# Attention and two expert layers on one core: the first chunk of expert 0 inside the attention stage, routing in groups of 4, 5, 5 and 4 token tiles with two under way

## The chip, the cores and the metric

The kernel runs on one core of one Trainium2 chip. The metric is the device time of one execution in microseconds; lower is better. TensorE (PE) multiplies and transposes, VectorE (DVE) and ScalarE (ACT) read and write the matmul memory PSUM, GpSimd (POOL) works between tiles in on-chip memory and issues gathers, and SyncE (SP) issues all other DMAs. Each engine runs its instructions in the order in which the program emits them.

## What is computed

An attention with pooled keys and values is followed by two mixtures of experts. The inputs are 4 batches, 8 heads, 576 positions and 64 dimensions, so 2304 tokens of 512 values.

```python
k_p = k.reshape(B, H, S//8, 8, D).mean(axis=3); v_p = the same of v
attn = softmax(q @ k_p.T / sqrt(D));  x = attn @ v_p        # [2304, 512]
noisy = x @ w_gate + log1p(exp(x @ w_noise)) * noise        # 8 experts
top2, weights = two largest of noisy, softmax over the two
out1[token] = sum over its two experts of weight * (relu(x @ w1[e]) @ w2[e])   # F = 1024
out2 = sum over 4 experts of p[:, e] * (relu(out1 @ w1b[e]) @ w2b[e])          # dense
```

## The kernel before

The attention works on 18 tiles of 128 tokens, each in two units of four heads, so 36 units; `LAG` is 5. Iteration `i` of the loop at line 651 emits for PE the scores of unit `i`, the transposes of the exponentials of unit `i - 2` and the values of unit `i - 5`. Between them `soft` emits for DVE the maximum of unit `i`, and the reciprocal and the products of unit `i - 6` (`normalise`: one product for x, one for the gate columns). The exponential is ACT's; in every fourth unit DVE first subtracts the maximum into the tile `sh`. After every tile its x goes to DRAM (`x_d`) and its gate logits to `lg`. Iterations 36 to 41 have no scores left; `warm` emits three filler matmuls in each of them (line 658).

`routing(g, hold)` (line 322) is a generator that turns the logits of a group of tiles into places in the experts' token lists: softplus noise, the two largest (`max`, `max_index`), one-hot tiles, counts by matmul (`pos`), positions, one-hot tiles again (`oh_hi` for the list's block, `oh_lo` for the row in it), and their product by matmul into a table (`tab`), which is added to `slotf`. Each `yield` ends one step; `step` (line 446) runs some steps of the first generator in the list `bg`, between the other work. The groups are tiles 0-3, 4-8, 9-11 and 12-17, one after another. A `yield` with a value holds the generator until that many further calls. After the second group the first two blocks of the lists of experts 0 and 1 are known (`slots[False]`), and POOL gathers their rows of `x_d` (`fetch1`, line 569). After the last group the others are fetched.

Then come the experts. A chunk of tokens is worked in two halves of F. Each half has four layer-1 units (line 718: 12 matmuls each, three terms of a split into high and low parts) and a layer-2 sum per 128 tokens (line 782: 12 matmuls of 512 columns). ACT writes the relu's high part, DVE the low part (`relu_split`). `run_plain` (line 817) runs a chunk; the first two chunks have 256 tokens, the first of expert 0 and of expert 1. Weights come in items of 512 KB: SP loads one into one of three staging tiles, ACT copies its high part and POOL (in some places DVE) subtracts for the low part (lines 506 to 518), into rings of three places for layer 1 and three for layer 2, the third of which lies in memory that the attention uses. Items 0 to 4 are split during the attention (line 643), the others beside the chunks (`ahead_plain`, line 795). `turn_plain` (line 587) turns gathered tiles with PE and splits them: ACT the high part, DVE the low part. At line 673 the attention's memory is closed and the tiles of the expert stage take its place.

What the steps of the prediction touch: the loop (651 to 668), `soft`, `transposes`, `normalise` (249 to 304), `routing` and `step` (322 to 455), `relu_split` and `layer1` (706 to 729), lines 669 to 673, and the first two calls of `run_plain` (955 to 962).

Of the kernel before, what the change touches and what calls it, by code (L numbers as in the profile page):

```python
# [22 lines left out]
J = S // POOL  # L23
# [12 lines left out]
GROUPS = (0, 4, 9, 12, NT)  # L36
EARLY = 2
LAG = 5
STEPS = (4, 4, 2, 3, 3, 5, 5, 4, 4)
GN = 6  # L40
# [15 lines left out]
def tile_attention_moe_moe(  # L56
# [93 lines left out]
    for t in et_sb:  # L150
# [7 lines left out]
                   base=0, channel_multiplier=0, allow_small_or_imprecise_dtypes=True)  # L158
    exp_i = consts.tile([128, E1], FT, name="exp_i")
# [75 lines left out]
    sps, es, ets, xs, lgm, pvs = {}, {}, {}, {}, {}, {}  # L235
# [13 lines left out]
    def soft(i, j):  # L249
# [21 lines left out]
    def transposes(i):  # L271
# [4 lines left out]
        nc.scalar.activation(ets[i][:J], p[:J], AF.Copy)  # L276
# [12 lines left out]
    def normalise(i, rec):  # L289
        t, g = divmod(i, 2)  # L290
        p3 = pvs[i]
        if g == 0:
            xs[t] = wk.tile([128, DM], FT, name="xs", bufs=6)
            lgm[t] = wk.tile([128, H, 2 * E1], FT, name="lgm", bufs=2)
        nc.vector.tensor_tensor(xs[t][:, g * 256:(g + 1) * 256].rearrange("p (h d) -> p h d", d=D),
                                p3[:, :, 0:D], rec.unsqueeze(2).to_broadcast([128, 4, D]), op=OP.mult)
        step()
        nc.vector.tensor_tensor(lgm[t][:, 4 * g:4 * g + 4, :], p3[:, :, D + 1:VW],
                                rec.unsqueeze(2).to_broadcast([128, 4, 2 * E1]), op=OP.mult)
        step()  # L300
        if g == 1:
            nc.sync.dma_start(x_d[t * 128:(t + 1) * 128, :], xs[t])
            nc.vector.tensor_reduce(lg[:, t, :], lgm[t].rearrange("p h c -> p c h"),
                                    axis=AX.X, op=OP.add)
# [16 lines left out]

    def routing(g, hold):
# [5 lines left out]

        def w(name, c=E1, d=FT):
            return consts.tile([128, GN, c], d, name="g_" + name)[:, :n]  # L330
# [7 lines left out]
        yield  # L338
        nc.scalar.activation(ln, u, AF.Ln)
# [3 lines left out]
        nc.vector.tensor_scalar(u, z, 0.0, None, op0=OP.max)  # L343
        yield
        nc.vector.tensor_sub(ln, ln, d)
        yield
        nc.vector.tensor_add(ln, ln, u)
# [19 lines left out]
        yield hold[0]  # L367
        pos = psr.tile([128, 512], FT, name="tr")
# [14 lines left out]
        nc.vector.tensor_add(base, base, cnt)  # L383
        yield
# [17 lines left out]
        lo = consts.tile([128, GN, 2, 128], HF, name="oh_lo")[:, :n]  # L402
        hi = consts.tile([128, GN, 2, HC], HF, name="oh_hi")[:, :n]
# [15 lines left out]
        yield hold[3]  # L419
        if a:  # L420
# [13 lines left out]
        if g == EARLY - 1:  # L434
            nc.vector.tensor_tensor(base, base, least, op=OP.max)
            yield
        if last:
            nc.vector.tensor_reduce(top_n, base, axis=AX.X, op=OP.max)
            nc.vector.tensor_scalar(over, top_n, float(CAP), None, op0=OP.is_gt)
            yield  # L440

    bg = []

    held = [0]
# [179 lines left out]

    at(2, pool_v, 0)
# [14 lines left out]
    at(28, make_va, 3)  # L640
    for g in range(len(GROUPS) - 2):
# [473 lines left out]
```

## Time and profile before

| | us |
|---|---|
| median of 3 runs | 1330.58 |
| lowest, highest | 1327.60, 1330.93 |
| the profiled execution | 1331.74 |
| its span, first to last instruction | 1329.90 |

All durations below are of that one profiled execution. Its last scores start at 83.39 us after the span's start, the first chunk's layer 1 at 104.92, the second chunk at 129.14 and the third at 161.39. In the views, "idle" is time in which an engine had nothing to run, with what ended it; the granted clock is a share of TensorE's 2.4 GHz, the lower of its two levels being 1.2 GHz, so a mean between 0.5 and 1 is a mix of both. Matmuls overlap at their ends: the distance from one group's start to the next says what the first costs.

### The profile page before, as it was taken

How to read it: one execution, taken by the hardware profiler on the slowest of the kernel's cores; microseconds unless marked ns; L12 is line 12 of the kernel's file. 1: busy time of each engine (PE TensorE's matmuls, PEld its weight loads, DVE VectorE, ACT ScalarE, POOL GpSimd, SP SyncE). 2: the span in 40 equal slices, each digit the busy share in tenths (PEclk: the TensorE clock that was granted, in tenths of full speed). 3: DMA queues.
4: the chain of work that ended last, by engine and by line, in shares of the span. 5: the costliest groups of instructions: out<-in, count | busy, mean ns of one | idle time of the engine just before them, and what ended most of it. 6: DMA issues, size and time to landing. Idle time of an engine off the chain costs nothing.

```text
span 1329.9 us, 19627 instructions
## 1 busy us (share of the span) xinstructions
PE 1302.2 (98%) x7430; PEld 1160.0 (87%) x7430; DVE 729.4 (55%) x1361; ACT 571.1 (43%) x1039; POOL 848.2 (64%) x761
## 2 busy tenths in 40 slices
PE   8898999999999999999999999999999999999998
PEld 6767898899889988898888998999999889999997
DVE  6886525475675732567545457545444574444444
ACT  6754445556454544554433334434333433333331
POOL 6725588897977945423967666767566566655560
PEclk9999999999999999999999999999999999999999
DMA  9643565342424424663333223323221232222211
GB/s 364 220 144 93 162 201 179 110 153 95 150 96 136 156 90 131 218 205 119 115 95 94 81 64 118 121 64 111 73 70 64 64 111 74 70 72 71 64 33 48
DMA packets 48805, 156.19 MB, mean 117 GB/s; under 512 B 5952, under 2 KB 7744, under 8 KB 47552
## 3 DMA queue, kind: packets, MB, share of 16 engines
q1 hardware_dynamic: 42624, 134.94, 30.9%
q0 software_dynamic: 6080, 19.93, 4.7%
q8 instruction: 61, 1.00, 0.3%
q14 instruction: 40, 0.33, 0.1%
HBM read 134.92 MB, written 19.92 MB: 116 GB/s over the span
## 4 chain that ended last, share of the span: by engine, by line
PE 57%; DVE 3%; ACT 1%; DMA 0%; issue 0%; ACTq 0%; DVEq 0%
PE p L789 29%; PE wn L743 23%; PE wn L726 4%; DVE x L618 1%; PE tr L577 1%; DVE acc L1029 0%; DMA gat<-y_d,rows 0%; ACT hs L709 0%; ACT x L615 0%; DVE hs L710 0%; DVE gat L885 0%; DVE sx L607 0%; DVE wn L773 0%; DVE wn L764 0%; DVE v L518 0%
## 5 line engine op out<-in xcount | busy, mean ns | idle before, releaser
L743 PE MATMUL wn<-x,u 128*128 128x384 f32 (+1 forms) x2688 | 452.4, 327 | 0.2 <-ACT u L755 0.2
L743 PEld LDWEIGHTS wn<-x,u 128*128 128x128 f32 x2688 | 445.5, 188 | 2.9 <-ACT u L755 0.4
L789 PE MATMUL p<-v,hs 128*128 128x512 f32 x1776 | 438.4, 393 | 3.5 <-ACT hs L709 2.0
L789 PEld LDWEIGHTS p<-v,hs 128*128 128x128 f32 x1776 | 329.9, 188 | 75.6 <-ACT hs L709 4.5
L709 ACT ACTIVATE hs<-wn 128x384 fp32r<-128x384 f32 (+2 forms) x320 | 147.1, 468 | 280.9 <-DVE wn L764 146.2
L789 PE MATMUL p<-v_last,hs 128*128 128x512 f32 x912 | 235.0, 393 | 0.8 <-DVE acc L1029 0.5
L710 DVE SCALAR_TENSOR_TENSOR hs<-wn,hs 128x384 fp32r<-128x384 f32 (+2 forms) x320 | 163.9, 528 | 128.9 <-ACT hs L709 122.2
L789 PEld LDWEIGHTS p<-v_last,hs 128*128 128x128 f32 x912 | 170.9, 189 | 36.8 <-DVE acc L1029 1.0
L1029 DVE SCALAR_TENSOR_TENSOR acc<-p,pe,acc 128x512 f32<-128x512 f32 x126 | 94.5, 750 | 188.8 <-PE p L789 186.6
L518 POOL TENSOR_TENSOR v<-w_st,v 128x1024 fp32r<-128x1024 f32 x41 | 101.8, 2484 | 120.9 <-ACT v L512 120.8
L541 POOL TENSOR_TENSOR u<-comb,u 128x1024 fp32r<-128x1024 f32 x60 | 149.6, 2494 | 44.6 <-ACT u L535 44.2
L533 POOL TENSOR_TENSOR u<-w_st,u 128x768 fp32r<-128x768 f32 x60 | 114.0, 1900 | 49.1 <-ACT u L527 49.1
L512 ACT ACTIVATE v<-w_st 128x1024 fp32r<-128x1024 f32 x64 | 67.5, 1056 | 168.6 <-PE p L789 165.4
L726 PE MATMUL wn<-x,u 128*128 128x384 f32 (+1 forms) x768 | 125.0, 320 | 1.6 <-DVEq L1001 1.4
L726 PEld LDWEIGHTS wn<-x,u 128*128 128x128 f32 x768 | 120.9, 193 | 3.9 <-issue 1.8
L516 POOL TENSOR_TENSOR u<-w_st,u 128x256 fp32r<-128x256 f32 x80 | 59.6, 776 | 52.4 <-ACT u L512 32.0
L518 POOL TENSOR_TENSOR v_last<-w_st,v_last 128x1024 fp32r<-128x1024 f32 x22 | 55.2, 2510 | 47.9 <-ACT v_last L512 47.9
L535 ACT ACTIVATE u<-comb 128x1024 fp32r<-128x1024 f32 x64 | 67.5, 1054 | 29.1 <-POOL comb L525 29.1
L758 DVE TENSOR_TENSOR u<-wn,u 128x384 f32<-128x384 f32 (+1 forms) x64 | 34.4, 537 | 73.9 <-PE wn L743 39.2
L522 POOL TENSOR_TENSOR comb<-w_st 128x256 f32<-128x256 f32 x64 | 49.6, 775 | 36.2 <-DMA w_st<-wb 34.1
L512 ACT ACTIVATE v_last<-w_st 128x1024 fp32r<-128x1024 f32 x32 | 33.7, 1055 | 78.1 <-PE p L789 75.0
L565 POOL DMA_INDIRECT gat<-y_d,rows x36 | 36.9, 1026 | 36.7 <-DVE hs L710 13.6
(142 smaller groups left out, 1317.5 us busy)
## 6 DMA issues: line engine op xcount, KB each, us to landing
w_st<-wb SPq DMA_DIRECT2D x104, 512.0 KB
w_st<-wa SPq DMA_DIRECT2D x88, 512.0 KB
y_d<-acc SPq DMA_DIRECT2D x40, 256.0 KB
x_d<-xs SPq DMA_DIRECT2D x18, 256.0 KB
out<-acc SPq DMA_DIRECT2D x18, 256.0 KB
k_st<-kt SPq DMA_DIRECT2D x3, 1152.0 KB
v_st<-vt SPq DMA_DIRECT2D x3, 1152.0 KB
q_sb<-qt SPq DMA_DIRECT2D x3, 1152.0 KB
```

Of the source, the lines that this page charges most:

```text
L512: nc.scalar.activation(w[:, 0], st, AF.Copy)
L516: eng.tensor_sub(w[:, 1, i], st[:, i], w[:, 0, i].bitcast(FT))
L518: eng.tensor_sub(w[:, 1], st, w[:, 0].bitcast(FT))
L533: nc.gpsimd.tensor_sub(w[:, 1, 0:3], st[:, 1:4], w[:, 0, 0:3].bitcast(FT))
L535: nc.scalar.activation(w[:, 0, 3:7], t, AF.Copy)
L541: nc.gpsimd.tensor_sub(w[:, 1, 3:7], t, w[:, 0, 3:7].bitcast(FT))
L709: nc.scalar.activation(hi, p, AF.Relu)
L710: return lambda: nc.vector.scalar_tensor_tensor(hs[:, 1, f, c0:c0 + n], p, 0.0, hi.bitcast(FT), op0=OP.max, op1=OP.subtract)
L726: nc.tensor.matmul(p, w[:, a, qu, (kd % 2) * 128:(kd % 2 + 1) * 128], xc[(xa, xb)[kd // 2]][:, b, kd % 2, :n], start=i == 0, stop=i == 11)
L743: nc.tensor.matmul(p, w[:, a, wm, kd * 128:(kd + 1) * 128], xc[xm][:, b, kd, :n], start=first and i == 0, stop=i == 5, skip_group_check=True)
L789: nc.tensor.matmul(p, hs[:, a, f, t * 128:(t + 1) * 128], w[:, b, f % 2], start=f == 0 and i == 0, stop=f == FB // 2 - 1 and i == 2)
L1029: nc.vector.scalar_tensor_tensor(a, p, w, a, op0=OP.mult, op1=OP.add)
```

## The change

- Groups are tiles 0-3, 4-8, 9-13 and 14-17. `step` may go on with a second group while the first is held; a turn counter keeps their sums in order, and odd and even groups have work tiles of their own. More steps are taken in each iteration (`STEPS`), and holds last one call.
- `LAG` is 4. In every fourth unit the exponential is taken by the copy after the transposes. From tile 6 on x and gate columns are one product, and x is stored from a tile whose rows hold them side by side, 64 values of every 81.
- Routing's absolute value is ACT's, log(1 + e) is one ACT instruction with a bias, and two DVE instructions are merged into one.
- The first two gathered tiles of expert 0 are turned in iteration 35. The first four layer-1 units stand between the values of iterations 36 to 39 in place of the fillers. Layer 2 and the second half follow the loop, with a routing step of six after each; the result of both halves is summed in PSUM. Weight items 5 to 9 are split there. The last group starts right after the loop.
- The attention's memory is closed after that chunk. The second chunk reads its x from other tiles, and `run_plain` is called for it first. `combine_weights` becomes the end of the last group.

```diff
-GROUPS = (0, 4, 9, 12, NT)
+GROUPS = (0, 4, 9, 14, NT)
-LAG = 5
-STEPS = (4, 4, 2, 3, 3, 5, 5, 4, 4)
-GN = 6
+LAG = 4
+STEPS = (4, 4, 5, 5, 6, 7, 7, 6, 6)
+GN = (5, 5)
+JOINED = 6
...
-                sh = wk.tile([128, 4, J], FT, name="sh")
-                nc.vector.tensor_sub(sh, sps[i], mx.unsqueeze(2).to_broadcast([128, 4, J]))
-                nc.scalar.activation(es[i], sh, AF.Exp)
+                nc.vector.tensor_sub(es[i], sps[i], mx.unsqueeze(2).to_broadcast([128, 4, J]))
...
-        nc.scalar.activation(ets[i][:J], p[:J], AF.Copy)
+        nc.scalar.activation(ets[i][:J], p[:J], AF.Copy if i % 4 else AF.Exp)
...
+        if t >= JOINED:
+            x = xs[t].rearrange("p (h c) -> p h c", c=VW)
+            gates, x = x[:, :, D + 1:VW], x[:, :, 0:D]
+            nc.vector.tensor_tensor(xs[t].rearrange("p (h c) -> p h c", c=VW)[:, 4 * g:4 * g + 4, :], p3,
+                                    by.to_broadcast([128, 4, VW]), op=OP.mult)
...
-            nc.sync.dma_start(x_d[t * 128:(t + 1) * 128, :], xs[t])
+            nc.sync.dma_start(x_d[t * 128:(t + 1) * 128, :].rearrange("p (h d) -> p h d", d=D), x)
...
-        nc.vector.scalar_tensor_tensor(az, z, -1.0, z, op0=OP.mult, op1=OP.max)
-        yield
+        nc.scalar.activation(az, z, AF.Abs)
         nc.scalar.activation(ex, az, AF.Exp, scale=-1.0)
-        yield
+        nc.scalar.activation(ln, ex, AF.Ln, bias=one)
+        yield 0 if last else 1
...
+        while turn["base"] != g:
+            yield 1
...
-        while bg and n:
-            try:
-                if held[0]:
-                    held[0] -= new
-                    return
-                held[0] = next(bg[0]) or 0
-                n -= 1
-            except StopIteration:
-                bg.pop(0)
+        for r in list(bg):
+            if held.get(r):
+                held[r] -= new
+                continue
+            while n and not held.get(r):
+                try:
+                    held[r] = next(r) or 0
+                    n -= 1
+                except StopIteration:
+                    bg.remove(r)
+                    break
...
+    def first1(q, f):
+
+        layer1(q, f, S1, S2, FIRST, lambda: ps.tile([128, 512], FT, name="s"), h_first[q])
+        w_at["used1"] += f % 2
+
+    def first2(q, i):
+
+        if not y_first:
+            y_first.extend(ps.tile([128, 512], FT, name="et") for _ in range(FIRST // 128))
+        s = 4 * q + 2 + i
+        w_check(s)
+        w = w_slot(s)
+        for f in range(2):
+            for t in range(FIRST // 128):
+                for j, (a, b) in enumerate(TERMS):
+                    nc.tensor.matmul(y_first[t], h_first[q][:, a, 2 * i + f, t * 128:(t + 1) * 128], w[:, b, f],
+                                     start=q == i == f == j == 0, stop=q == i == f == 1 and j == 2,
+                                     skip_group_check=True)
+        w_at["used2"] += 1
+
+    def first_out(t):
+        y = wk.tile([128, H * VW], FT, name="xs", bufs=5)[:, 0:DM]
+        nc.scalar.activation(y, y_first[t], AF.Copy)
+        nc.sync.dma_start(y_d[t * 128:(t + 1) * 128, :], y)
...
+    for c in range(FIRST // 128):
+        at(35, turn_plain, (0, c), (S1, S2), c)
...
-        at(2 * GROUPS[g + 1] + LAG, lambda g=g: bg.append(routing(g, ((2, 1, 6, 1), (2, 1, 1, 1), (2, 1, 2, 1))[g])))
+        at(2 * GROUPS[g + 1] + LAG, lambda g=g: bg.append(routing(g, (1, 1, 1, 1))))
...
-        if i >= NI:
-            warm(3, ps, "s")
         if LAG <= i < NI + LAG:
             values(i - LAG)
+        if NI <= i < NI + 4:
+            first1(0, i - NI)
...
-    until(lambda: False in slots)
-    for c in range(FIRST // 128):
-        turn_plain((0, c), (S1, S2), c)
-    warm(4, ps, "s")
+    bg.append(routing(len(GROUPS) - 2, (1, 1, 1, 1)))
+    w_whole(5)
+    first2(0, 0)
+    step(6, 1)
+    first2(0, 1)
+    step(6, 1)
+    for f in range(FB // 2):
+        first1(1, f)
+        step(6, 1)
+        if f < 2:
+            w_whole(6 + f)
+        else:
+            turn_plain((1, f - 2), (A22, S4), f - 2)
+    for i in range(2):
+        first2(1, i)
+        w_whole(8 + i)
+        step(6, 1)
+    for t in range(FIRST // 128):
+        first_out(t)
+    until(lambda: turn["done"] > EARLY)
     att.close()
...
-    bg.append(routing(len(GROUPS) - 2, (3, 1, 1, 2)))
-    bg.append(combine_weights())
...
-    for c in range(2):
-        add(0, 1 + c, turn_plain, (1, c), (A11, S3), c)
-    run_plain(S1, S2, FIRST, sink1(0, 0), fills, 7)
-    fills.clear()
...
-        add(1, 3 + c, turn_plain, (0, 2 + c), (A22, S4), c)
-    run_plain(A11, S3, FIRST, sink1(1, 0), fills, 7, nc.gpsimd, nc.vector)
+        add(1, 3 + c, turn_plain, (0, 2 + c), (A11, S3), c)
+    run_plain(A22, S4, FIRST, sink1(1, 0), fills, 7, nc.gpsimd, nc.vector)
...
-    run_plain(A22, S4, CA, sink1(0, FIRST), fills)
+    run_plain(A11, S3, CA, sink1(0, FIRST), fills)
```

## Rows read from the trace of the kernel before

**Rows 1.** Stretches: length, busy PE, PEld, DVE, ACT, POOL (instructions), granted clock, DMA share, GB/s.
```profile
50.00:100.00 50.00, 43.15 (x552) 33.55 (x547) 41.66 (x174) 29.54 (x90) 20.38 (x28) 0.97 0.42 133
...
130.00:139.00 9.00, 5.30 (x34) 4.52 (x33) 6.97 (x13) 1.64 (x4) 1.79 (x3) 0.65 0.62 193
...
161.00:1329.00 1168.00, 1158.79 (x6063) 1045.32 (x6061) 615.03 (x962) 479.91 (x784) 762.87 (x621) 1.00 0.33 106
83.40:161.40 78.00, 69.01 (x499) 56.34 (x498) 47.93 (x170) 30.73 (x64) 34.96 (x46) 0.91 0.38 125
```

**Rows 2.** One stretch, the filler matmuls of line 465 alone: PE, PEld, clock, DMA.
```profile
83.40:161.40 78.00, 7.41 (x22) 2.19 (x22) 0.91 0.38 125
```

**Rows 3.** PE in order of time: start, us, instruction; iterations 34 to 36.
```profile
81.55 0.76 PE L245 MATMUL s<-kb,q_sb 128*128 128x144 f32 x4
...
82.67 0.79 PE L284 MATMUL pv<-va,et 128*64 128x81 f32 x16
83.39 0.76 PE L245 MATMUL s<-kb,q_sb 128*128 128x144 f32 x4
...
86.97 0.79 PE L284 MATMUL pv<-va,et 128*64 128x81 f32 x16
```

**Rows 4.** PE in order of time, the first chunk.
```profile
104.92 1.86 PE L726 MATMUL wn<-x,u 128*128 128x256 f32 x12
...
111.96 5.74 PE L789 MATMUL p<-v,hs 128*128 128x512 f32 x24
117.54 5.91 PE L726 MATMUL wn<-x,u 128*128 128x256 f32 x48
...
129.14 1.59 PE L726 MATMUL wn<-x,u 128*128 128x256 f32 x12
```

**Rows 5.** PE in order of time, the second chunk and the third's start.
```profile
133.39 1.25 PE L417 MATMUL tr<-oh_hi,oh_lo 128*128 128x40 f16 x8 [2.66 <-DVE oh_lo L410]
...
135.74 6.20 PE L726 MATMUL wn<-x,u 128*128 128x256 f32 x36
...
147.85 4.47 PE L726 MATMUL wn<-x,u 128*128 128x256 f32 x36
152.16 0.60 PE L577 MATMUL tr<-ident,gat 128*128 128x128 f32 x4
152.51 1.68 PE L726 MATMUL wn<-x,u 128*128 128x256 f32 x12
...
161.39 2.79 PE L726 MATMUL wn<-x,u 128*128 128x384 f32 x15
```

**Rows 6.** DVE in order of time: one-hot tiles of two groups.
```profile
54.47 2.59 DVE L410 TENSOR_TENSOR oh_lo<-slot_i,g_sf 128x256 f16<-128x256 f16 x3
...
85.68 1.09 DVE L410 TENSOR_TENSOR oh_lo<-slot_i,g_sf 128x256 f16<-128x256 f16 x3
```

**Rows 7.** Groups of instructions: busy us, mean ns, idle before; DVE's gate product.
```profile
L298 DVE TENSOR_TENSOR lgm<-pv,rec 128x64 f32<-128x64 f32 x36 | 7.7, 214 | 0.0
```

**Rows 8.** POOL in order of time, weight splits of the first chunk.
```profile
113.62 2.82 POOL L516 TENSOR_TENSOR u<-w_st,u 128x256 fp32r<-128x256 f32 x4 [18.99 <-PE p L789]
...
120.58 2.85 POOL L516 TENSOR_TENSOR v<-w_st,v 128x256 fp32r<-128x256 f32 x4
```

**Rows 9.** ACT in order of time, the copy of a weight item as it lands.
```profile
127.38 1.06 ACT L512 ACTIVATE v<-w_st 128x1024 fp32r<-128x1024 f32 x1 [1.76 <-DMA w_st<-wa]
```

**Rows 10.** ACT in order of time, the splits of a turned tile.
```profile
100.09 0.38 ACT L584 ACTIVATE x<-tr 128x256 fp32r<-128x256 f32 x1 [7.56 <-PE tr L577]
101.03 0.38 ACT L584 ACTIVATE x<-tr 128x256 fp32r<-128x256 f32 x1 [0.56 <-DVE x L585]
```

**Rows 11.** Stretches as in rows 1, with the stores of two tiles.
```profile
98.00:100.00 2.00, 2.00 (x29) 1.40 (x29) 1.83 (x8) 0.00 (x0) 0.00 (x0) 1.00 0.34 131
100.00:101.00 1.00, 0.05 (x1) 0.00 (x0) 0.42 (x1) 0.38 (x1) 0.00 (x0) 1.00 0.68 262
```

**Rows 12.** Groups of instructions: ACT's table load.
```profile
L128 ACT ACT_TABLE_LOAD x1 | 1.3, 1283 | 0.7 <-PEq L1107 0.7
```

More of the change, by code (lines that the diff above doesn't have):

```diff
@@ L158, in tile_attention_moe_moe @@
                    base=0, channel_multiplier=0, allow_small_or_imprecise_dtypes=True)
+    one = consts.tile([128, 1], FT, name="one")
+    nc.vector.memset(one, 1.0)
     exp_i = consts.tile([128, E1], FT, name="exp_i")
@@ L383, in routing @@
         nc.vector.tensor_add(base, base, cnt)
+        if g == EARLY - 1:
+            nc.vector.tensor_tensor(base, base, least, op=OP.max)
+        turn["base"] += 1
         yield
@@ L419, in routing @@
         yield hold[3]
+        assert turn["slot"] == g
+        turn["slot"] += 1
         if a:
@@ L440, in routing @@
             yield
+            yield from combine_weights()
+        turn["done"] += 1
     bg = []
-    held = [0]
+    held = {}
     def step(n=1, new=0):
-        while bg and n:
-            try:
-                if held[0]:
-                    held[0] -= new
-                    return
-                held[0] = next(bg[0]) or 0
-                n -= 1
-            except StopIteration:
-                bg.pop(0)
+        for r in list(bg):
[9 more added lines that the diff above has]
+                    break
     def until(done):
@@ L622, in x_both, with relu_split, pair_weights, bank @@
         x_lo(m, n)
+    TERMS = ((0, 0), (0, 1), (1, 0))
+    hid = []
+    def relu_split(f, c0, n, p, hs=None):
+        hs = hs or hid[0]
+        hi = hs[:, 0, f, c0:c0 + n]
+        nc.scalar.activation(hi, p, AF.Relu)
+        return lambda: nc.vector.scalar_tensor_tensor(hs[:, 1, f, c0:c0 + n], p, 0.0, hi.bitcast(FT),
+                                                      op0=OP.max, op1=OP.subtract)
+    def pair_weights(q, pr):
+        s = 4 * q + pr
+        w_check(s)
+        return w_slot(s)
+    def bank():
+        return pm.tile([128, 512], FT, name="wn", bufs=4)
+    def layer1(q, f, xa, xb, n, bank=bank, hs=None):
+        w = pair_weights(q, f // 2)
+        p = bank()[:, :n]
+        i = 0
+        for a, b in TERMS:
+            for kd in range(KD):
+                qu = (0 if f % 2 else 1) if kd < 2 else (3 if f % 2 else 2)
+                nc.tensor.matmul(p, w[:, a, qu, (kd % 2) * 128:(kd % 2 + 1) * 128],
+                                 xc[(xa, xb)[kd // 2]][:, b, kd % 2, :n], start=i == 0, stop=i == 11)
+                i += 1
+        relu_split(f, 0, n, p, hs)()
+    h_first, y_first = [], []
+    def first1(q, f):
[5 more added lines that the diff above has]
+        s = 4 * q + 2 + i
+        w_check(s)
+        w = w_slot(s)
[10 more added lines that the diff above has]
+        nc.sync.dma_start(y_d[t * 128:(t + 1) * 128, :], y)
     at(2, pool_v, 0)
@@ L702, in combine_weights @@
         yield
-    TERMS = ((0, 0), (0, 1), (1, 0))
-    def relu_split(f, c0, n, p):
-        hi = hs[:, 0, f, c0:c0 + n]
-        nc.scalar.activation(hi, p, AF.Relu)
-        return lambda: nc.vector.scalar_tensor_tensor(hs[:, 1, f, c0:c0 + n], p, 0.0, hi.bitcast(FT),
-                                                      op0=OP.max, op1=OP.subtract)
-    def pair_weights(q, pr):
-        s = 4 * q + pr
-        w_check(s)
-        return w_slot(s)
-    def layer1(q, f, xa, xb, n):
-        w = pair_weights(q, f // 2)
-        p = pm.tile([128, 512], FT, name="wn", bufs=4)[:, :n]
-        i = 0
-        for a, b in TERMS:
-            for kd in range(KD):
-                qu = (0 if f % 2 else 1) if kd < 2 else (3 if f % 2 else 2)
-                nc.tensor.matmul(p, w[:, a, qu, (kd % 2) * 128:(kd % 2 + 1) * 128],
-                                 xc[(xa, xb)[kd // 2]][:, b, kd % 2, :n], start=i == 0, stop=i == 11)
-                i += 1
-        relu_split(f, 0, n, p)()
     def layer1_seven(q, pr, n, fills, u):
@@ L749, in go @@
                 f()
-        p1, p6, p7, p5 = (bank() for _ in range(4))
+        p1, p6, p7, p5 = (bank()[:, :n] for _ in range(4))
         s1, u2, u3 = (moe.tile([128, CA], FT, name=f"u{i}")[:, :n] for i in range(3))
```

47 lines of the change are left out of this document (23 added, 24 removed).

## The prediction

> **What bounds the kernel now.** I read the view of stretches first, to see where TensorE (PE) falls short. From the third chunk on (161 us to the end) PE is busy 1158.79 of 1168 us at a granted clock of 1.00; nothing is to be had there, and what this change moves lies ahead of that mark. From the last scores to that mark, 83.4 to 161.4, it is busy 69.01 of 78.00 us at a mean clock of 0.91 [rows 1], and 7.41 us of that are the filler matmuls that only keep it active [rows 2]. So 78 us are spent on about 55 us of wanted work. PE's order of time then says where. In iteration 35 the values start at 86.97, where the pace would give 84.5 [rows 3]. The first chunk's layer 1 starts only at 104.92 and the chunk ends at 129.14, nearly without a pause [rows 4]. The second chunk (129.14 to 161.39) holds a 2.66 us wait for DVE's one-hot tiles, and then 36 matmuls take 6.20 us that take 4.47 later, the clock being 0.65 over 130 to 139 [rows 1, 5]. That wait is group 3's routing. Everything here is measured between two marks: the scores of iteration 35 (83.39) and the first 384-column matmul of the third chunk (161.39), 78.0 us apart.
>
> **What PE has to do between the marks afterwards.** Iteration 35 without a wait is one pace, 83.39 - 81.55 = 1.84 us, of which the values are 83.39 - 82.67 = 0.72 [rows 3]. After it stand four values (2.9) and two sets of transposes (at most the pace less the values, 1.1 for both). Seven gathered tiles are turned, at 152.51 - 152.16 = 0.35 each: 2.5 [rows 5]. Chunks 1 and 2 are four halves: 48 layer-1 matmuls at the pace of 36 in 152.16 - 147.85 = 4.31, so 5.75 [rows 5], and 24 layer-2 matmuls in 117.54 - 111.96 = 5.58 [rows 4]; four times 11.33 is 45.3. Routing matmuls of two groups: 1.5, from one group's 8 in 1.25 [rows 5]. Sum 55.1. The fillers, six trailing iterations without other work, and the first chunk's standing alone are gone: 78.0 - 55.1 = 22.9 us if PE never waits. What it will wait for has to come off that.
>
> **The waits, part by part.**
> (a) Routing inside the attention. Counting the yields, group 1's slots come out in iteration 32 instead of 36, its one-hots in 28 and 29 instead of 34, and group 2 is at its counts by 35 instead of 39. The 2.1 us that iteration 35 lost (86.97 less 84.5 and its 0.33 of table matmuls) is DVE running late with group 1's one-hots [rows 3]; it moves ahead of the first mark. But there POOL is splitting weights: three one-hot instructions took 2.59 us beside POOL's split against 1.09 without [rows 6]. Ends: 0, if the gaps of the earlier iterations take it, to 4.2, twice the loss. I take 2.1. In the other direction 24 units lose DVE's small gate product, 0.21 us each [rows 7], for a longer joint one, and four groups lose two small DVE instructions: 0 to 1 us, taken as 0, since these iterations' DVE work is not what PE waits for in most of them.
> (b) Before the first unit. The two gathers are issued in iteration 32, three paces or 5.5 us before they are turned. The nearest landing in the trace is a 512 KB weight load: released by POOL's end at 123.43, its copy could start at 127.38, so 3.95 us [rows 8, 9]. That leaves 1.5 us, less if stores and loads share the engines; 0.7, ends 0 and 4.7. Then four splits alternate between ACT and DVE, 0.94 us apart (101.03 is 0.56 of waiting for DVE and then 0.38 [rows 10]): about 3.4 us, of which turning, transposes and values cover 1.6. That makes 1.8. Together 2.5, ends 0 and 6.5.
> (c) Clock. A stretch with waits of this size was followed by the lower level, 1.2 GHz, and 36 matmuls cost 6.20 - 4.47 = 1.7 us more [rows 5]. One such fall: 1.7; ends 0 and 3.4.
> (d) First chunk. Units 0 to 3 need weights that are split long before. Item 5 can be split once the loop is over: POOL has 18.99 us of idle time there now [rows 8]. Items 6 and 7 must wait for the first layer-2 steps to free their places and are split in 2.85 us each [rows 8], ready about 1.5 us before use. 0.8 for group 2's table and a late weight; ends 0 and 3.
> (e) Second chunk. Group 3's four one-hots run beside POOL's splits at 0.86 us each [rows 6] and their table is wanted by unit 3, after three units of 1.44: 1.9 us late, and 0.3 for a relu behind a weight copy. 2.2; ends 1 and 7.8, the present loss of this chunk (32.25 less 24.4).
> Costed at nothing: the output of the first chunk (two ACT copies of PSUM at its end; cover: the second chunk's first two units write other banks; price without it about 1 us, like the splits), the Abs on ACT, and w_load behind the stores on SP, which waits for POOL anyway.
> Waits 9.3 in all (1.0 to 24.9), gain 22.9 - 9.3 = **13.6 us**.
>
> **Two prices that no row shows.** From iteration 18 the stores of x leave in 256-byte pieces. Over 98 to 101 two stores held the 16 engines 0.68 us each [rows 11]. If a small piece cost as long as a 2 KB one, a store would take eight times that, 5.4 us; if its bytes decided, 0.68. The share of 0.42 over 50 to 100 leaves 29 us free [rows 1], 37 with the twelve present stores taken out, so they fit up to 3.1 us each. I take them to fit, as nearer to the lower end by bytes. The Trainium skill (DMA: Bandwidth & Descriptors, Specifications) wants 512 bytes or more for line rate, since a smaller write is read, modified and written; its section on why small descriptors are slow adds 27% for 256 bytes. By that page a store would take an estimated 2 x 1.27 x 0.68 = 1.7 us, twelve 21 us, and they would fit. A second: Abs stands in no row. If it switched ACT's table and back in each group, 8 loads of 1.28 us [rows 12] would be up to 10 us of ACT time, mostly beside PE work; the other end is 0, which I take because Relu, Copy, Exp and Ln already share the single load. The Trainium skill (ScalarE: Activation LUTs, Table sets: the hidden batching unit) lists abs among the functions that every set holds; by it the price is 0.
>
> **The rivals.**
> A, the waits as above: 13.6 us. B, PE hardly waits: DVE's savings and early gathers leave (b) at 1.8 and (e) at 1, gain about 20, 1310.6. For it: over 50 to 100 DVE is busy 41.66 of 50 us and ACT 29.54 [rows 1]. Against: DVE is the late engine wherever PE waits now.
> C, weights take the place of routing. Four items of 2.85 us of POOL per half are 11.4 [rows 8], and PE takes 11.33 per half: level. If item 6's late place leaves POOL idle for 4 us and three gathers (2.9) stand between its splits, the first two chunks are paced by POOL; 6.9 of the gain is lost, 1324.
> D, the other side: the stores of small pieces. Above 3.1 us each they no longer fit; at 5.4 the twelve need 65 us where 37 are free, and gathers and weights come 28 us late: 1317 + 28 = 1345. It begins to cost more than the gain at about 4.2 us a store. Against it: the share of bytes.
> E, the change doesn't do what it says: group 1 comes too late, so that the chunk doesn't fit between the last values. The late end of (b) costs 4.0 more, a second fall of the clock 1.7, group 3 that much later 1.9: gain 6.0, 1324.6.
>
> **How the numbers follow.** The profiled execution took 1331.74 us (span 1329.90, 1.84 around it), 1.16 above the median of 1330.58. Against its own time A gives 1331.74 - 13.6 = 1318.1; against the median 1317.0, which I give. A's own range is 1312 to 1322 (waits 5 to 14). Chances: A 0.58, B 0.12, C 0.14, E 0.08, D 0.08. The range is 1309 to 1326: A, B and most of C and E, leaving out D and their ends. A measurement of this kernel tells 0.3%, 4 us, from no change, so faster means below 1326.6: A, B, 0.09 of C, 0.05 of E make 0.84; the remains of C and E, 0.08, are the same; D, 0.08, is slower.
>
> **What would show it.** After: layer-1 matmuls between the values of iterations 32 to 35; no filler at the end; the third chunk's first 384-column matmul 56 to 70 us after the scores of iteration 35, about 64. (a) scores of iteration 35 near 85.5; (b) PE's wait ahead of its first unit, 1 to 3 us, named after the gather or the split; (e) a wait for one-hots under 2.5 us in chunk 2. The prediction is wrong if the attention itself grows by more than 4 us, if SP or DMA are busy above 0.9 between 50 and 100, if ACT loads a second table, or if PE waits for items 6 to 13. From the third chunk on nothing should change; if it does, the premise of the marks has failed.

## The result: 1.4% slower

| | us |
|---|---|
| before, median of the executions timed beside it | 1330.21 |
| after, median (lowest, highest) | 1348.70 (1345.14, 1353.09) |
| after to before | 1.0144, interval 1.0109 to 1.0180 |
| the profiled execution of after, its span | 1347.00, 1345.10 |
| forecast (range) | 1317.0 (1309 to 1326) |

The change was to make the kernel faster by 13.6 us; it made it slower by some 18, and the interval leaves no doubt of the sign. In the views below, `hs` is the relu's output, which layer 2 reads; `u` are weights of layer 1, `v` and `v_last` those of layer 2 (`v_last` is the third place of its ring); `acc` are the running sums. The profile after, first by stretches (columns as in [rows 1]):

```profile
87.10:158.10 71.00, 59.87 (x450) 52.78 (x449) 44.85 (x143) 31.75 (x65) 35.38 (x46) 0.95 0.46 140
50.00:100.00 50.00, 43.01 (x538) 37.02 (x539) 39.48 (x153) 31.98 (x98) 21.99 (x30) 0.93 0.49 128
130.00:139.00 9.00, 3.12 (x22) 3.01 (x19) 2.56 (x5) 2.08 (x5) 4.32 (x6) 0.74 0.59 184
158.00:1345.00 1187.00, 1173.90 (x6062) 1049.63 (x6060) 612.32 (x961) 481.23 (x783) 760.90 (x618) 1.00 0.33 104
```

PE in order of time, the end of the attention (answers [rows 3, 4]):

```profile
87.10 0.76 PE L248 MATMUL s<-kb,q_sb 128*128 128x144 f32 x4
...
89.13 0.54 PE L285 MATMUL pv<-va,et 128*64 128x81 f32 x9 [0.84 <-DVE rec L259]
...
93.27 0.50 PE L667 MATMUL s<-x,u 128*128 128x256 f32 x2 [0.66 <-ACT x L599]
94.20 0.98 PE L667 MATMUL s<-x,u 128*128 128x256 f32 x6 [0.43 <-ACT x L599]
```

PE in order of time, the second chunk and the third's start (answers [rows 5]):

```profile
136.06 0.25 PE L429 MATMUL tr<-oh_hi,oh_lo 128*128 128x40 f16 x2 [5.88 <-DVE oh_lo L422]
136.14 2.91 PE L667 MATMUL wn<-x,u 128*128 128x256 f32 x12
...
145.51 4.47 PE L667 MATMUL wn<-x,u 128*128 128x256 f32 x36
...
158.16 8.64 PE L667 MATMUL wn<-x,u 128*128 128x384 f32 x48
```

The first mark, the scores of iteration 35, came at 87.10 (83.39 before), the second at 158.16 (161.39). So the third chunk starts only 3.2 us earlier. Then comes what the prediction had ruled out: from the second mark to the end it is 1345.1 - 158.2 = 1186.9 us against 1329.9 - 161.4 = 1168.5, 18.4 us more. Together -3.2 + 18.4 = 15.2, the difference of the two spans. The last stretch says of what kind: PE is busy 1173.90 of 1187 us where it was busy 1158.79 of 1168 [rows 1], with as many instructions (6062 and 6063) and the same mean granted clock of 1.00. So 15.1 us are in longer matmuls and 3.9 in waits. The groups of PE's instructions from the third chunk on (busy us, mean ns, idle before them), after:

```profile
L810 PE MATMUL wn<-x,u 128*128 128x384 f32 (+1 forms) x2688 | 455.2, 328 | 1.0 <-DVE u L828 0.6 <-ACT u L822 0.3
L856 PE MATMUL p<-v,hs 128*128 128x512 f32 x1706 | 430.1, 398 | 2.3 <-ACT hs L647 1.3 <-DVE hs L648 0.7 <-DVE acc L1090 0.2
L856 PE MATMUL p<-v_last,hs 128*128 128x512 f32 x888 | 229.8, 394 | 0.3 <-DVE acc L1090 0.3
L667 PE MATMUL wn<-x,u 128*128 128x384 f32 (+1 forms) x576 | 100.9, 333 | 5.0 <-DVEq L1062 5.0
```

and before:

```profile
L743 PE MATMUL wn<-x,u 128*128 128x384 f32 (+1 forms) x2688 | 452.4, 327 | 0.2 <-ACT u L755 0.2
L789 PE MATMUL p<-v,hs 128*128 128x512 f32 x1707 | 420.9, 392 | 3.0 <-ACT hs L709 1.5 <-DVE hs L710 0.9 <-DVE acc L1029 0.5
L789 PE MATMUL p<-v_last,hs 128*128 128x512 f32 x888 | 228.5, 393 | 0.5 <-DVE acc L1029 0.5
L726 PE MATMUL wn<-x,u 128*128 128x384 f32 (+1 forms) x576 | 98.5, 327 | 1.4 <-DVEq L1001 1.4
```

Layer 2 from `v` is 9.2 us longer for as many matmuls, the other three groups 6.5 together; and one wait, for DVE at the branch that tests the overflow flag, went from 1.4 to 5.0 us. Three things are thus to be explained: the pace, the branch, and the 5.88 us wait for `oh_lo` in the second chunk.

### The profile page after: what moved, and what is told of

It is laid out like the page before. It is cut to its first block, busy times and chain, and to the rows that moved or that the text cites. A ratio compares the mean times of both kernels' runs of the same rounds, so it can differ in the third digit from the quotient of the medians.

```text
span 1345.1 us, 19514 instructions
## 1 busy us (share of the span) xinstructions
PE 1311.4 (97%) x7408; PEld 1164.3 (87%) x7408; DVE 725.4 (54%) x1328; ACT 571.6 (42%) x1034; POOL 848.7 (63%) x759
## 4 chain that ended last, share of the span: by engine, by line
PE 58%; DVE 2%; ACT 1%; issue 0%; ACTq 0%; DVEq 0%
PE p L856 30%; PE wn L810 24%; PE wn L667 4%; DVE x L633 1%; PE tr L592 1%; DVE acc L1090 0%; ACT hs L647 0%; ACT x L630 0%; DVE hs L648 0%; ACT gat L949 0%; DVE u L533 0%; DVE wn L831 0%; ACT u L527 0%; DVE wn L840 0%; DVE x L600 0%
## 5 line engine op out<-in xcount | busy, mean ns | idle before, releaser
L810 PE MATMUL wn<-x,u 128*128 128x384 f32 (+1 forms) x2688 | 455.2, 328 | 1.0 <-DVE u L828 0.6
L810 PEld LDWEIGHTS wn<-x,u 128*128 128x128 f32 x2688 | 447.8, 188 | 4.6 <-DVE u L828 0.9
L856 PEld LDWEIGHTS p<-v,hs 128*128 128x128 f32 x1740 | 324.4, 189 | 79.7 <-DVE hs L648 3.6
L648 DVE SCALAR_TENSOR_TENSOR hs<-wn,hs 128x384 fp32r<-128x384 f32 (+2 forms) x312 | 160.5, 531 | 134.3 <-ACT hs L647 124.7
L856 PEld LDWEIGHTS p<-v_last,hs 128*128 128x128 f32 x900 | 168.0, 188 | 39.2 <-DVE acc L1090 0.8
L556 POOL TENSOR_TENSOR u<-comb,u 128x1024 fp32r<-128x1024 f32 x60 | 149.8, 2496 | 46.4 <-ACT u L550 46.3
L667 PE MATMUL wn<-x,u 128*128 128x384 f32 (+1 forms) x672 | 114.5, 328 | 5.0 <-DVEq L1062 5.0
L667 PEld LDWEIGHTS wn<-x,u 128*128 128x128 f32 x672 | 110.9, 194 | 6.5 <-issue 5.3
```

The costliest lines, as they stand in the source:

```text
L556: nc.gpsimd.tensor_sub(w[:, 1, 3:7], t, w[:, 0, 3:7].bitcast(FT))
L648: return lambda: nc.vector.scalar_tensor_tensor(hs[:, 1, f, c0:c0 + n], p, 0.0, hi.bitcast(FT), op0=OP.max, op1=OP.subtract)
L667: nc.tensor.matmul(p, w[:, a, qu, (kd % 2) * 128:(kd % 2 + 1) * 128], xc[(xa, xb)[kd // 2]][:, b, kd % 2, :n], start=i == 0, stop=i == 11)
L810: nc.tensor.matmul(p, w[:, a, wm, kd * 128:(kd + 1) * 128], xc[xm][:, b, kd, :n], start=first and i == 0, stop=i == 5, skip_group_check=True)
L856: nc.tensor.matmul(p, hs[:, a, f, t * 128:(t + 1) * 128], w[:, b, f % 2], start=f == 0 and i == 0, stop=f == FB // 2 - 1 and i == 2)
```

## The experiments

All ratios are against the kernel before, timed beside each (its medians there are 1328 to 1330 us). The kernels a_... are the changed kernel with one or more edits, b_... the kernel before with one.

| kernel | us, median | ratio, interval | third chunk starts | from there to the end |
|---|---|---|---|---|
| before | 1329 | 1 | 161.4 | 1168.5 |
| after | 1348.7 | 1.0144 (1.0109 to 1.0180) | 158.2 | 1186.9 |
| a_pad928 | 1336.6 | 1.0048 (1.0028 to 1.0068) | 159.7 | 1174.7 |
| a_pad32 | 1345.2 | 1.0103 (1.0079 to 1.0128) | 161.1 | 1185.1 |
| b_pad32 | 1339.8 | 1.0071 (1.0051 to 1.0092) | 159.0 | 1178.7 |
| a_free | 1350.5 | 1.0135 (1.0101 to 1.0170) | 162.2 | 1187.2 |
| a_pad160 | 1333.8 | 1.0039 (1.0021 to 1.0057) | 152.8 | 1174.6 |
| a_edge480 | 1333.6 | 1.0030 (1.0013 to 1.0046) | 153.7 | 1174.3 |
| a_dve31 | 1325.6 | 0.9975 (0.9962 to 0.9989) | 157.0 | 1168.1 |
| a_best3 | 1328.3 | 0.9986 (0.9968 to 1.0004) | 158.5 | 1167.9 |
| a_best5 | 1331.5 | 1.0012 (0.9998 to 1.0027) | 161.1 | 1168.1 |
| a_best4 | 1325.0 | 0.9961 (0.9948 to 0.9975) | 156.0 | 1168.3 |
| b_hs32 | 1341.8 | 1.0096 (1.0078 to 1.0115) | 159.0 | 1180.4 |
| b_dve97 | 1335.4 | 1.0050 (1.0032 to 1.0067) | 160.0 | 1174.5 |

The last two columns are of one profiled execution each. The first of them varies by up to 8 us between kernels whose program is alike up to there (after, a_pad928, a_pad32, a_pad160, a_edge480, a_dve31); the second repeats within 0.7 us where nothing in it differs, so it carries the comparisons.

### Where the tiles of the expert stage lie

The compiled programs give the addresses. Of routing's work tiles, those that lie among the constants have room for five token tiles instead of six (`GN`), 960 bytes less in all, and a tile of 32 bytes was added; so every tile of the expert stage's pool, which begins behind them (`v_last`, `x0`, `hs`, `acc`), lies 928 bytes lower: `hs` at 81248 instead of 82176. The tiles at the other end (`u` and `v` of the weights, `x1`, `x3`) have not moved.

```diff
     moe = pool(ctx, "moe", 1)
+    moe.tile([128, 232], FT, name="pad")      # a_pad928; [128, 8] in a_pad32
```

> The changed kernel with one unused tile of 928 bytes a partition at the start of the expert stage's pool, so that v_last, x0, hs and the other tiles of that pool lie at the addresses that they have in the kernel before (hs at 82176 instead of 81248). Theory T1, that the pace of the matmuls from the third chunk on depends on where these tiles lie: layer 2 of that stretch goes back from 235.2 to about 229.4 ns a matmul, the stretch from the third chunk's first matmul to the end from 1186.9 to about 1169.5 us, and the time to about 1331 us, 1.3% under the changed kernel. Rival R2, that the pace comes from something else of the change (its order of work, its transfers): the pace stays at 235 ns and the time at about 1348 us.

> The same with a pad of 32 bytes only: the tiles lie 896 bytes below those of before, hs at 81280, again on multiples of 64 bytes. T1 in its narrow form, that a start at an odd multiple of 32 bytes is what slows them: 229.4 ns and about 1331 us, as with 928 bytes. Rival R1, that the distance from other tiles or from some boundary larger than 64 bytes counts: the pace stays slow, or goes back in part, and the time lies between 1335 and 1348 us. R2: 1348 us.

In the kernel before, the same line with 8 elements:

> The kernel before with a pad of 32 bytes at the start of the expert stage's pool and nothing else: its tiles start at odd multiples of 32 bytes (hs at 82208). T1 in its narrow form: layer 2 from 229.4 to about 235 ns a matmul, and the time up by about 17 us, to 1347. R1: between 1331 and 1340 us, as far as 32 bytes move a distance. R2: no change, 1330 us.

With before's addresses layer 2 is back to before's pace, here in a_pad928,

```profile
L857 PE MATMUL p<-v,hs 128*128 128x512 f32 x1708 | 420.9, 392 | 2.8 <-ACT hs L647 1.5 <-DVE hs L648 0.7 <-DVE acc L1091 0.5
```

and 12.2 us are gained behind the mark. So R2 falls. (The 1336.6 instead of 1331 is the branch below, which in that execution kept PE for 6.65 us.) The narrow form of T1 falls too: 32 bytes put the starts on multiples of 64 again, and the pace stays slow. And the kernel before loses 10.2 us by 32 unused bytes alone. The groups of b_pad32 from 161 us on:

```profile
L744 PE MATMUL wn<-x,u 128*128 128x384 f32 (+1 forms) x2688 | 452.7, 328 | 0.1
L790 PE MATMUL p<-v,hs 128*128 128x512 f32 x1704 | 429.1, 398 | 2.6 <-ACT hs L710 1.4 <-DVE hs L711 0.9 <-DVE acc L1030 0.2
L790 PE MATMUL p<-v_last,hs 128*128 128x512 f32 x888 | 230.6, 395 | 0.3 <-DVE acc L1030 0.3
```

That left two theories, the remainder of the start's own address by 256 and the distance between the tiles of the two ends:

```diff
+    moe.tile([128, 40], FT, name="pad")       # a_pad160
-EDGE = 248
+EDGE = 480                                    # a_edge480
```

> The changed kernel with an unused tile of 160 bytes at the start of the expert stage's pool: its tiles lie 768 bytes under those of the kernel before (hs at 81408, v_last at 29184), again on multiples of 256 bytes, while the buffers of the other side (v0 at 211968, u0 at 168960) stay where they are in both kernels. Theory that the start's remainder by 256 bytes sets the pace: layer 2 of the third chunk and after at 229.4 ns a matmul as with 928 bytes, about 1336 us. Rival, that it is the distance between the tiles of the two sides that counts: not the distance of before, so the pace stays at 233 to 236 ns, about 1346 us.

> The changed kernel with the tiles of the other side (x3, x1, the buffers u and v of the weights) moved down by 928 bytes too, through a longer unused tile at that side's end. All distances between tiles of the expert stage are those of the kernel before; all of their starts leave 160 or 96 bytes by 256 instead of nothing. Theory of the remainder: the pace stays slow, 231 ns or more for layer 2, and the weight tiles now add their own, 1346 us or above. Rival of the distance: 229.4 ns, about 1336 us.

Layer 2 of a_pad160:

```profile
L857 PE MATMUL p<-v,hs 128*128 128x512 f32 x1704 | 420.0, 392 | 2.9 <-ACT hs L647 1.6 <-DVE hs L648 0.7 <-DVE acc L1091 0.5
L857 PE MATMUL p<-v_last,hs 128*128 128x512 f32 x888 | 228.6, 393 | 0.5 <-DVE acc L1091 0.5
```

and of a_edge480:

```profile
L856 PE MATMUL p<-v,hs 128*128 128x512 f32 x1704 | 419.9, 392 | 2.9 <-ACT hs L647 1.6 <-DVE hs L648 0.7 <-DVE acc L1090 0.5
L856 PE MATMUL p<-v_last,hs 128*128 128x512 f32 x888 | 227.6, 391 | 0.5 <-DVE acc L1090 0.5
```

Both are fast, and each theory as I had put it is refuted by one of them: starts that are no multiple of 256 are harmless if all are moved alike (a_edge480), and another distance is harmless if it differs by a multiple of 256 (a_pad160 by 768). What is left is the distance's remainder by 256. To see which tile, in the kernel before:

```diff
+    moe.tile([128, 8], FT, name="pad")
     hs = moe.tile([128, 2, FB // 2, CW], FR, name="hs")
```

> The kernel before with 32 unused bytes just ahead of hs, so that hs, acc and the three work tiles of the seven-product layer lie 32 bytes further, while v_last and all tiles of x stay. With all tiles of that pool moved by 32 bytes the time rose from 1329.4 to 1339.8 us, layer 2 from 229.1 to 234.5 ns (231.4 with v_last), the layer-1 products with x3 and its neighbours from 173.3 to 174.7, and those with x0 not at all. If hs against the weight tiles of the other side sets the pace: layer 2 with v rises to 234 ns as there, and about 9 us are lost. If it is the operands x and v_last: no change, 1329 us.

```profile
L744 PE MATMUL wn<-x,u 128*128 128x384 f32 (+1 forms) x2688 | 452.4, 327 | 0.0
L790 PE MATMUL p<-v,hs 128*128 128x512 f32 x1704 | 429.0, 398 | 2.6 <-ACT hs L710 1.3 <-DVE hs L711 0.9 <-DVE acc L1030 0.2
L790 PE MATMUL p<-v_last,hs 128*128 128x512 f32 x886 | 232.7, 398 | 0.3 <-DVE acc L1030 0.3
```

Layer 1 is untouched to 0.1 us, and layer 2 is slow with both its weight tiles, since now neither has `hs`'s remainder. So it goes by where `hs` lies to the weights; `acc` and three work tiles of layer 1 moved along, but they are read and written by other engines, and another engine is not the cause. Of the distances between neighbours of layer 2 with `v` that have no instruction of ACT, DVE or POOL and no transfer beside them (61 in either kernel), the mean is 226.7 ns before and 233.2 in b_hs32. The distance from one layer-2 matmul's start to the next (mean of the neighbours under 330 ns, from 300 us on) sums it up, with two layer-1 products beside it, one whose x lies in the expert pool (S3) and one whose x lies at the other end (S1):

| kernel | `hs` less `v0`, remainder by 256 | `v` | `v_last` | S3 | S1 |
|---|---|---|---|---|---|
| before, a_pad928, a_pad160, a_edge480, a_dve31, a_best3, a_best4, a_best5, b_dve97 | 0 | 229.1 to 229.2 | 228.4 to 228.5 | 173.3 | 173.3 |
| b_hs32 | 32 | 234.5 | 233.9 | 173.3 | 173.3 |
| b_pad32 | 32 | 234.5 | 231.4 | 173.2 | 174.6 |
| after | 96 | 234.8 | 231.3 | 176.1 | 173.9 |
| a_pad32 | 128 | 233.7 | 231.0 | 176.8 | 173.2 |

Not settled is why `v_last`, which moves with `hs`, still loses half where the whole pool moves, and why in b_pad32 it is S1 that suffers, whose operands have not moved, and not S3. So the rule by `hs` and `v` describes layer 2 with `v` and is not the whole. In after and a_edge480 `v_last` and `hs` have the same addresses, and the pace with `v_last` is 231.3 and 228.5 ns; what differs is where `v` and the other tiles of the far end lie, which these matmuls do not read. No run tells how that reaches them.

### The branch

At the test of the overflow flag DVE compares and jumps over the code of the rare case. Its own instructions at that line, before and after (count, durations, start):

```profile
L1001 DVEq COMPARE_BRANCH  x1: 72/72/72, 507.7 to 507.7; - x1
L1001 DVEq EVENT_SEMAPHORE  x1: 21/21/21, 508.3 to 508.3; - x1
```

```profile
L1062 DVEq COMPARE_BRANCH  x1: 72/72/72, 507.7 to 507.7; - x1
L1062 DVEq EVENT_SEMAPHORE  x1: 21/21/21, 511.8 to 511.8; - x1
```

From the branch to DVE's next instruction it is 0.52 us before and 4.05 after. The programs count 829 instructions of DVE ahead of the branch before, 798 after; the jump is 167 long in both. It costs more than the wait: in after the granted clock over 505 to 515 us is 0.74, where it is 1.00 before, and the 48 matmuls behind the branch take 10.6 us from first to next start where they take 8.4. So of the 18.4 us some 5.7 are the branch, and of the 15.1 us of longer matmuls 2.2 are its.

```diff
     for e in range(2, E1 - 1):
         fills.clear()
+        if e == 2:
+            for j in range(31):                                            # a_dve31, on top of the pad of 928
+                add(j // 16, j % 16, nc.vector.memset, pad[:, j:j + 1], 0.0)
```

> The changed kernel with the pad of 928 bytes and 31 more one-column writes by VectorE, one a step in the third expert's chunk, so that VectorE has as many instructions ahead of the branch on the overflow flag (829) as in the kernel before; the changed kernel has 798. In the kernel with the pad alone the branch keeps VectorE for 5.75 us (0.52 before), PE waits 6.7 us for it and then works at the lower clock. Theory T3, that the branch's length hangs on where it stands in VectorE's instruction stream: VectorE goes on after about 0.5 us, PE waits 1.4 us, and the time falls by 5 to 7 us against the pad alone, to 1329 to 1331 us. Rival, that it comes from something else at that moment, such as the transfers under way: the wait stays at 5 to 7 us and the time at 1336 us.

In b_dve97 the same stands in the kernel before, three writes a step, on the tile `edge`:

> The kernel before with 97 more one-column writes by VectorE, three a step in the third expert's chunk, on an unused tile; all addresses stay. VectorE then has 926 instructions ahead of the branch on the overflow flag, 128 more than the 798 of the changed kernel, where the branch kept it for 4.05 us; before it has 829 and the branch keeps it for 0.52. Theory T3 with a period of 128 instructions, which is a guess: the branch keeps VectorE for 4 to 6 us, PE waits for it 5 us instead of 1.4 and then runs at the lower clock, and the time rises by 4 to 6 us to about 1335. If the position counts without that period, or if the length comes from something that only the changed kernel has: 0.5 us, and a time of 1330, or up to 2 us more where the writes themselves delay VectorE.

PE's first matmuls behind the branch, in the order before, after, a_dve31, b_dve97:

```profile
508.44 8.56 PE L726 MATMUL wn<-x,u 128*128 128x384 f32 x48 [1.43 <-DVEq L1001]
```

```profile
511.97 10.23 PE L667 MATMUL wn<-x,u 128*128 128x384 f32 x45 [4.96 <-DVEq L1062]
```

```profile
504.31 8.56 PE L667 MATMUL wn<-x,u 128*128 128x384 f32 x48 [1.43 <-DVEq L1066]
```

```profile
511.37 10.09 PE L726 MATMUL wn<-x,u 128*128 128x384 f32 x48 [5.51 <-DVEq L1004]
```

T3 holds, in both directions, and in every profile: the gap is 0.52 us in all seven kernels with 829 instructions and 4.05 to 5.75 in the seven others (798, 926, and 799 in a_free). With 829 instructions the changed kernel's branch costs 0.52 us again, and from the third chunk to the end it takes 1168.1 us; with 926 the kernel before pays 4.6 us there and 1.5 more for 48 matmuls behind it, and is 0.5% slower. The guess of a period of 128 came true once. Where between 799 and 829 the limit lies was not tried. The packets of the queue that the page calls `q14 instruction` show what differs. In each of the seven kernels with 829 one of them moves 10.4 to 10.8 us ahead of the branch; here are the transfers of before from 497 to 498 us:

```profile
q14 instruction: 1, 0.01, 1.9%
```

In the seven others none moves at that distance, and one more moves behind the branch: four within 7 us, where it is three with 829, the first 2.2 to 3.1 us behind the branch and 1.8 to 2.8 before DVE goes on. That fits a wait for instructions that are fetched late; the fetch was not varied by itself. With pad and count in place the change is the faster kernel, by 0.25%; all 18.4 us behind the second mark are accounted for. The step from a_pad928 to a_dve31 in the table, 11 us, holds 6.6 of this; the rest lies ahead of the mark, in the part that varies.

### The first chunk's output

The chain behind the 5.88 us wait, in the changed kernel: ACT copies the output from PSUM into two buffers `xs`, then has to write `hs`;

```profile
125.06 1.29 ACT L696 ACTIVATE xs<-et 128x512 f32<-128x512 f32 x2 [1.77 <-PE et L689]
...
134.83 0.66 ACT L647 ACTIVATE hs<-wn 128x256 fp32r<-128x256 f32 x2 [4.63 <-DMA y_d<-xs]
```

SP stores the two buffers, queued behind four weight loads;

```profile
129.18 0.85 SPq L697 DMA_DIRECT2D y_d<-xs  x2
```

and on DVE the last one-hot tile stands behind the relu that needs ACT's half:

```profile
135.25 0.42 DVE L648 SCALAR_TENSOR_TENSOR hs<-wn,hs 128x256 fp32r<-128x256 f32 x1 [5.37 <-ACT hs L647]
135.59 0.42 DVE L422 TENSOR_TENSOR oh_lo<-slot_i,g_sf 128x256 f16<-128x256 f16 x1
```

The buffers lie at 101472 and 104064, the first inside what becomes `hs` (81248 to 105824), the second across its end. To move them out:

```diff
+    kept = [wk.tile([128, H * VW], FT, name="xs", bufs=5) for _ in range(3)]
+    for k in kept:
+        nc.gpsimd.memset(k[:, 0:8], 0.0)
     for t in range(FIRST // 128):
         first_out(t)
```

> The changed kernel with three of the five buffers named xs held back through three tiles that only have 8 elements written, so that the output of the first chunk is written into buffers that lie above hs (which ends at 105824) instead of inside it. Theory T2, that the second chunk's wait of 5.88 us for oh_lo comes from VectorE's first use of hs behind the store of the first chunk's output: the write of hs at 134.83 goes at about 130.2, the wait falls to 1 to 2 us, the clock in the second chunk's first units stays up, the third chunk starts 5 to 8 us earlier, at 150 to 153, and the time falls to about 1341. Rival, that VectorE's own chain of routing is late: the wait stays above 4 us and the time at 1348. The pace of the later matmuls stays slow in either case.

```profile
134.72 0.22 PE L429 MATMUL tr<-oh_hi,oh_lo 128*128 128x40 f16 x2 [1.32 <-DVE oh_lo L422]
...
152.37 1.11 PE L592 MATMUL tr<-ident,gat 128*128 128x128 f32 x4 [5.60 <-DMA gat<-x_d,slots]
```

The wait falls to 1.3 us, as T2 says, and nothing is won, where I had expected 1341 us: PE arrives 5.6 us too early for the rows of the third chunk. POOL issued their gathers at 145.1 us (143.5 in after, whose PE turns them only at 149.8), since there they stand behind splits of weights. The wait had hidden the next one. The run that joined everything,

```diff
-            w_step(4 * q + i, n, eng2 if i in (3, 6) else eng)
+            w_step(4 * q + i, n, eng2 if i in (3, 6) or (q, i) == (2, 5) else eng)
```

> All of it together: the pad of 928 bytes, VectorE's 829 instructions ahead of the branch, the first chunk's output in buffers outside hs, and the low part of the weights of the second chunk's second half (the second pair) on VectorE instead of POOL, so that the gathers behind it on POOL are issued some 3 to 4 us earlier. Theory: PE's wait for oh_lo in the second chunk stays at 1.3 us, the wait of 5.6 us for the gathered rows of the third chunk falls to 0 to 2 us, the third chunk starts at 152 to 156 instead of 158 to 162, and from there to the end 1168 to 1171 us as before: 1321 to 1327 us, under the kernel before (1329.4). Rival, that the second chunk is bound by its weights whoever splits them: the wait moves to the weights or to VectorE, the third chunk starts at 158 or later, and the time is 1328 us or more.

was spoiled by the pad: with `hs` back at 82176 it ends at 106752, 96 bytes inside the buffer at 106656, and ACT waited as before:

```profile
135.09 0.66 ACT L647 ACTIVATE hs<-wn 128x256 fp32r<-128x256 f32 x2 [4.30 <-DMA y_d<-xs]
```

An overlap of 96 bytes brings back the whole wait (5.57 us for PE). With the pad of 160 there is none. a_best5 has POOL do the split, a_best4 DVE:

> The changed kernel with the pad of 160 bytes, 829 instructions of VectorE ahead of the branch, and three of the buffers xs held back, so that the first chunk's output lies at 106656 to 111840. With this pad hs ends at 105984, ahead of that output; in the run that joined all parts it ended at 106752, 96 bytes inside it, and the wait of 5.6 us for oh_lo was there. Theory T2, that the wait comes from hs standing behind the store of whatever it shares memory with: it falls to 1 to 2 us; PE then waits up to 5.6 us for the gathered rows of the third chunk, as in the run with the buffers held back alone, so the third chunk starts no more than 2 us earlier than at 157.0, and the time is 1324 to 1327 us. Rival, that the 96 bytes had no part in it: the wait stays above 5 us, 1325.6 us.

> The same with the low part of one weight tile of the second chunk's second half on VectorE instead of POOL. Theory: the gathers of the third chunk's rows leave POOL 3 us earlier and PE waits for them 0 to 2 us; with the wait for oh_lo at 1 to 2 us the third chunk starts at 150 to 154, and with 1168 us from there the time is 1319 to 1323 us, near the forecast of 1317. Rival, that weights and gathers together hold POOL too long whichever is first: a wait of 4 us or more for gathers or weights, the third chunk at 156 or later, 1325 us or more.

POOL in a_best5:

```profile
141.12 2.83 POOL L531 TENSOR_TENSOR u<-w_st,u 128x256 fp32r<-128x256 f32 x4 [1.51 <-ACT u L527]
144.10 1.92 POOL L580 DMA_INDIRECT gat<-x_d,slots  x1
```

POOL in a_best4, and PE:

```profile
143.63 0.97 POOL L580 DMA_INDIRECT gat<-x_d,slots  x1 [3.23 <-DVE top_n L449]
```

```profile
134.41 0.22 PE L429 MATMUL tr<-oh_hi,oh_lo 128*128 128x40 f16 x2 [1.32 <-DVE oh_lo L422]
...
147.65 0.66 PE L592 MATMUL tr<-ident,gat 128*128 128x128 f32 x4 [1.11 <-DMA gat<-x_d,slots]
...
155.98 1.23 PE L667 MATMUL wn<-x,u 128*128 128x384 f32 x6
```

In a_best5 the wait for `oh_lo` is 1.3 us and the one for the gathers 5.7; in a_best4 both are small. Between these two, which differ in that one split (and two of the writes that keep the count at 829), lie 6.5 us of median: what the early output is worth only once the gathers are early too. They did not become so as I had expected, by leaving POOL 3 us earlier. With the split on DVE the lists are ready later, POOL waits 3.23 us for them, and the first gather starts 0.5 us earlier; but its issue takes 0.97 us instead of 1.92, and from 145 to 148 us the gathers move 0.52 MB, where in a_best5 none of theirs moves before 148. Why the issue is shorter was not tried. a_best4 has the lowest median here, 0.39% under the kernel before, though its interval overlaps that of a_dve31. Its 1325.0 is above the 1319 to 1323 that I expected, and a_best5's 1331.5 above 1324 to 1327: between the scores of iteration 35 and the end of the first unit PE stood 3.5 and 3.3 us, where a_dve31 stood 1.3, with the same program in that stretch. Why it sometimes stands there is open, and one profile of each does not explain the 5.9 us of median between a_dve31 and a_best5; the early output alone is not shown to gain anything.

## Why the prediction was wrong, step by step

The sum was 22.9 us saved less 9.3 waited. Its main error is not in it.

- **"From the third chunk on nothing should change."** This is the step that failed: it cost 18.4 us where nothing was put down and no reason given, 12.7 of it addresses and 5.7 the branch with the slower matmuls behind it (a_dve31 takes both back, to 1168.1). The rival of the other side, D, had the right sign and the wrong mechanism, and its 1345 lies near the measured 1348.7 by luck: the stores in small pieces held nobody up, no wait for a gather or a weight load stands between 87 and 158 us, and the engines' share over 50 to 100 went only from 0.42 to 0.49.
- **"Costed at nothing: the output of the first chunk."** I priced the two ACT copies and the PSUM banks, not the memory they are written to and the store that must leave it. The wait for `oh_lo` in the second chunk is 5.88 us, and 12 matmuls behind it take 2.7 instead of 1.5. This is most of (e), put at 2.2.
- **(a) Routing inside the attention**, 2.1: the first mark came 3.7 later. This execution has one long wait for DVE there, in PE's order of time,

```profile
52.91 1.35 PE L285 MATMUL pv<-va,et 128*64 128x81 f32 x16 [3.06 <-DVE xs L299]
```

and a granted clock of 0.66 in the ten us around it:

```profile
50.00:60.00 10.00, 7.09 (x64) 6.50 (x65) 8.36 (x18) 4.67 (x13) 9.39 (x14) 0.66 0.16 41
```

So there is a fall of the clock ahead of the marks, which the sum did not have. In a_edge480, the same program there, the clock stayed at 1.00 in that stretch and the scores of iteration 35 came 4 us earlier than in after; but a_dve31, with 0.83, came as late (87.3). Over the six kernels alike up to there that mark lies between 82.7 and 87.3 us, so the size of (a) is uncertain and its cause open.
- **What PE has to do**, 55.1: 59.9 were measured between the marks. Of the difference 2.3 are **(c)**, put at 1.7: one fall of the clock between the marks, to a mean of 0.74 over 130 to 139, with 12 matmuls of layer 1 and 6 of layer 2 slower right behind the wait. The other 2.5 are work that the sum had too short, 1.4 of it in the four halves and 0.6 in routing.
- **(b)** 2.5: 2.2 in all (0.84 + 0.24, 0.66 + 0.43), near the sum partly by luck. The splits cost 1.1 where 1.8 was put; there was no wait for gathers, put at 0.7; and 1.1 is mostly a wait for DVE's reciprocal ahead of the values, which (b) did not have.
- **(d)** 0.8: 2.9, of which 1.8 is the table of group 2, whose one-hots came one by one.
- **Abs**: right; ACT has the one table load of [rows 12] and no other.

Between the marks that is 71.1 us where the sum said 62.3. With the 1.6 of (a) the front end fell short by 10.4 of its 13.6 us. So the sum was also too hopeful by itself, in (e) and (d) above all: a kernel without the two effects behind the mark would by these marks have been some 0.25% faster and not 1%, which is what a_dve31 measures.

## What to carry to other kernels

Before saying that a stage is untouched, compare where its tiles lie and how many instructions each engine has ahead of its next branch: an edit hundreds of microseconds earlier moves both. A buffer costs the time until its last reader is done, and if a later tile takes its memory, that tile's first writer pays, even for 96 bytes. And a wait taken away shows the next one: price both together.

## What the runs showed of the hardware that I had not expected

- 32 unused bytes ahead of one tile cost 0.96% (b_hs32): a 128x512 matmul went from 392 to 398 ns by where `hs` lies to the weights, remainder 0 by 256 bytes being fast in all nine kernels that have it, 32, 96 and 128 slow in all five. The Trainium skill (SBUF — State Buffer, SBUF: two separate sides) says that on the engines' side only the port that VectorE and GpSimd share causes contention; by that the pace would not move with addresses. These rows say that it does, and without another engine at work beside it (226.7 against 233.2 ns), and the measurement decides.
- A branch of 0.5 us costs 4 to 6 us by where it stands in DVE's program (0.52 us at 829 instructions, 4.05 at 798, 4.61 at 926), with a period that fits 128 instructions. The Trainium skill (Runtime: NRT & Kernel Launch, Instruction fetch mechanics) says that a taken branch whose target is not loaded waits for a fetch, and gives blocks of 16 KiB, 256 instructions. The wait agrees; the block seems half as long for DVE here. The page of the profile has two queues of instructions: 0.97 MB in 59 packets are 16.4 KB each, 0.33 MB in 40 packets 8.2 KB, and it is the second whose packets move with DVE's branch.

```profile
q8 instruction: 59, 0.97, 0.3%
q14 instruction: 40, 0.33, 0.1%
```
